# Scores, convolution and output weights of a fused attention and gated MLP kernel, rearranged

## Chip, core and metric

The kernel runs on one core of one Trainium2 chip. The metric is device time in microseconds; three runs of the kernel before gave 685.39, 685.6 and 686.19 us, median 685.6.

## The reference, cut to what matters

Eight batches, each of 576 positions. Local attention over 8 heads of 64, then a gate made by a causal convolution of 5 taps, then a spatial MLP:

```python
scores = (q @ k.T) / sqrt(64)          # heads 0-3: keys 0..31 back; heads 4-7: every 4th key, 0..127 back
attn = softmax(where(mask, scores, -1e9))
x = attn @ v                            # [8, 576, 512], heads side by side
gate_pre = sum(conv_w[k] * x shifted by 4 - k positions for k in range(5))
x = (sigmoid(gate_pre) * (x @ moe_w_val)) @ moe_w_out
h = relu(x @ moe2_w_in); u, v = halves of h
v = layernorm(v over channels)
y = (u * (w_spatial @ v + b_spatial)) @ moe2_w_out
```

## The kernel before

**Layout.** The features lie on partitions, 128 at a time, the 576 positions in the free dimension. Heads go in pairs: pair p (0 to 3) holds two heads, one in partitions 0 to 63, one in 64 to 127. The positions of heads 4 to 7 are permuted on the host so that their dilated window is a plain one of 32. A pair has 18 query blocks of 32, and each needs 64 keys only.

**Scores** (`a_scores`, L278): for each of the 18 blocks and each head one matmul with 64 rows of contraction, 32 query columns and 64 keys, float32. Block `BLOCK[e][x]` goes to block column x (0 to 8) and partition half e of one PSUM tile `s_ps` with one buffer; head h goes to partitions 64 e + 32 h. So four positions of the array are used: rows 0 to 63 with column strips 0 and 64, rows 64 to 127 with strips 32 and 96. `a_max` (L295) adds the mask on VectorE, out of PSUM, and takes the maxima; `a_exp`, `a_sum` and `a_trans` finish the softmax. Behind the first batch `a_trans` (L341) transposes 32x32 blocks on VectorE and moves them into the tile `pt` with 16 transfers on SP's queue, by the four runs of block columns in `RUNS` (L38).

**PV and convolution.** `a_pv` (L380) multiplies `pt` with the values into the PSUM tile `o_ps` (one buffer, two banks), and ScalarE copies it to `xt`, which has four zero columns in front. `a_split` makes two float32r parts of `xt` for the products. `a_conv` (L413) makes the gate's input on VectorE, one `tensor_scalar` (L425) and four `scalar_tensor_tensor` (L427), each reading `xt` shifted by one more position. For pairs 2 and 3 the copy also undoes the permutation.

**MLP.** A batch has 37 steps on TensorE (`mlp_steps`, L461): 8 `val`, 5 `vstep`, 8 `ustep`, 8 `spstep` (spatial), 8 `outstep`. Each accumulates products of float32r parts into one of four PSUM buffers of the tag `m`, which VectorE or ScalarE must drain before it is used again. `spstep` is drained by VectorE (`ru`, L569). Each `vstep` puts its result in a buffer of the tag `v`, of which there are two; `vnorm` releases it, one step later. The last spatial matmuls of a step use the fifth v tile.

**Weights.** They come as float64. `load_w` brings them in, `from64` (L621) makes float32 of them with one ScalarE and four VectorE instructions, and a split makes two parts with one ScalarE cast and one GpSimd subtraction. The output weights `wo` come in four tiles through four buffers of the tag `raw`, which hold the spatial weights before; their float32 form uses the two buffers of tag `v`.

**Order.** `PRELUDE` lists what comes first. `FIRST` (L112) gives the weight work of the first batch a place among the 37 steps, and `attention_events` (L444) gives the attention of the next batch its places: PV of pair n stands at `pv_place(n)`, the scores two PVs ahead, the split 1 step behind PV (4.3 for pair 0), the convolution 0.2 behind that. All events are sorted by place and traced in that order. A scheduler then orders each engine's instructions by this order and by when it reckons operands and buffers to be ready; from the second batch on, matmuls stay in the order traced, and `in_order` pins an instruction behind the one traced before it on its engine. Queues of the engines and of SP are static: an instruction that waits holds up those behind it.

Of the kernel before, what the change touches and what calls it, by code (L numbers as in the profile page):

```python
# [8 lines left out]
F32 = mybir.dt.float32  # L9
# [23 lines left out]

BLOCK = [
    [3 * x if x < 6 else 3 * (x - 6) + 1 for x in range(NS)],
    [3 * (x + 3) + 1 if x < 3 else 3 * (x - 3) + 2 for x in range(NS)],
]
RUNS = [(0, 0, 6), (0, 6, 9), (1, 0, 3), (1, 3, 9)]  # L38

SCALE = 1.0 / float(D) ** 0.5  # L40

# [89 lines left out]
    (11.6, ("split_sp", 3)),  # L131
    (11.61, ("split_sp", 1)),
    (11.7, ("split_sp", 4)),
    (12.6, ("load_w", "wo", 0)),
    (14.2, ("w_f32", "wo", 0)),
    (14.21, ("split_out", "wo", 0)),
    (15.2, ("w_f32", "wo", 1)),
    (15.21, ("split_out", "wo", 1)),
    (15.3, ("load_w", "wo", 1)),
    (17.2, ("w_f32", "wo", 2)),  # L140
    (17.21, ("split_out", "wo", 2)),
    (18.2, ("w_f32", "wo", 3)),
    (18.21, ("split_out", "wo", 3)),
]


# [5 lines left out]
def attention_gated_mlp_kernel(  # L152
# [71 lines left out]
    def chunk(c):  # L224
        return slice(c * 128, c * 128 + 128)

    def by_slot(ap):
        return ap.rearrange("p (j k) -> p j k", k=SW)

    qk_t, vv_t, early = {}, {}, {}
    s_t, e_t, mx_t, sm_t, x_t, tt = {}, {}, {}, {}, {}, {}
    xh, xl = {}, {}

    def early_tile(p):
# [41 lines left out]
    def a_scores(b, p):  # L278
        t = qk_t.pop((b, p))
        s = ps_s.tile([128, 1024], F32, tag="s", name="s_ps")  # L280
        for i in range(2 * NS):
            x, e = divmod(i, 2)
            n = BLOCK[e][x]
            cols = slice(SW * x, SW * x + SW)
            keys = slice(QB * n, QB * n + SW)
            for h in range(2):
                r = slice(64 * h, 64 * h + 64)
                q = t[r, KEYS + QB * n:KEYS + QB * n + QB]
                o = 64 * e + QB * h
                matmul(s[o:o + QB, cols], q, t[r, keys], True, True)  # L290
        if b or p >= 2:
            load_qk(b, p + 2)
        s_t[b, p] = s

    def a_max(b, p):  # L295
        s = s_t.pop((b, p))
        if b == 0 and p == 1:
            e = by_slot(boot[:, 0:S])
        elif b == 0 and p == 2:
            e = by_slot(act.tile([128, S + 64], F32, tag="gh0", name="e_t")[:, 0:S])  # L300
        else:
            e = act.tile([128, NS, SW], F32, tag="e", name="e_t")
        in_order(b == 1 and p < 2, nc.vector.tensor_tensor(
            out=e, in0=by_slot(s[:, 0:S]), in1=mask_sb[:, p // 2], op=ALU.add
        ))
        mx = rot.tile([128, NS, 1], F32, tag="mx", name="mx")
        nc.vector.tensor_reduce(out=mx[:, :, 0], in_=e, axis=AX.X, op=ALU.max)
        if b < 2:
            nc.vector.tensor_scalar(out=mx, in0=mx, scalar1=-SCALE, scalar2=None, op0=ALU.mult)
            mx_t[b, p] = mx  # L310
        else:
            nc.vector.tensor_tensor(out=e, in0=e, in1=mx.to_broadcast([128, NS, SW]), op=ALU.subtract)
        e_t[b, p] = e
# [27 lines left out]
    def a_trans(b, p):  # L341
# [30 lines left out]
        for q, lo, hi in RUNS:  # L372
            j, i = divmod(BLOCK[q][lo], 3)
            for c in range(2):
                k = 32 * (i + c)
                for h in range(2):
                    r = 64 * q + 32 * h
                    nc.sync.dma_start(out=pt[k:k + 32, i, h, j:j + hi - lo], in_=t[r:r + 32, c, lo:hi])  # L378

    def a_pv(b, p):  # L380
# [8 lines left out]
        for j in range(NJ):  # L389
            c = 512 * (j // 3) + 96 * (j % 3)  # L390
            for h in range(2):
                r = slice(64 * h, 64 * h + 64)
                matmul(o[r, c:c + 96], u[:, j, r], pt[:, :, h, j], True, True)
        o = o.rearrange("p (a c) -> p a c", a=2)[:, :, 0:HS]
        if b or p >= 2:
            load_vv(b, p + 2)
        if p < 2:
# [14 lines left out]

    def a_conv(b, p):  # L413
        xt = x_t.pop((b, p))
        t = act.tile([128, S], F32, tag=f"tt{p}", name="tt")
        tt[b, p] = t
        if b == 0 and p == 0:

            nc.scalar.activation(out=t, in_=xt[:, 0:S], func=ACTF.Copy, scale=cw[:, p, 0:1])
# [196 lines left out]
    def in_order(late, ins):  # L616

        if late:
            tc.keep_in_program_order(ins)

    def from64(dst, src, late=False):  # L621


        hi, lo = src[..., 1], src[..., 0]
        di = dst.bitcast(I32)
        nc.scalar.activation(out=dst, in_=_f(hi), func=ACTF.Abs)
        in_order(late, nc.vector.tensor_scalar(
            out=dst, in0=dst, scalar1=LEAST, scalar2=MOST, op0=ALU.max, op1=ALU.min
        ))
        nc.vector.tensor_scalar(  # L630
            out=di, in0=di, scalar1=3, scalar2=0x3FFFFFF8, op0=ALU.logical_shift_left, op1=ALU.bitwise_and
        )
        nc.vector.scalar_tensor_tensor(
            out=di, in0=hi, scalar=-0x40000000, in1=di, op0=ALU.bitwise_and, op1=ALU.bitwise_or
        )
        nc.vector.scalar_tensor_tensor(
            out=di, in0=lo, scalar=29, in1=di, op0=ALU.logical_shift_right, op1=ALU.bitwise_or
        )

    def conv_w_f32():  # L640
        from64(cw.rearrange("p c k -> p (c k)"), cw_raw)
# [1 line left out]
    def w_f32(key, u):  # L643
        if key == "wo":
            wide[key, u] = rot.tile([128, DM], F32, tag="v", name="wo_f32")
            from64(wide[key, u], raw.pop((key, u)))
            return
        if key not in wide:
            if key == "wv":
# [182 lines left out]
```

## Time and profile before

| | |
|---|---|
| median of three runs | 685.6 us (685.39 to 686.19) |
| the profiled execution, span from first to last instruction | 682.8 us |
| TensorE busy | 655.3 us (96%) |
| VectorE busy | 433.5 us (63%) |
| ScalarE busy | 301.1 us (44%) |
| GpSimd busy | 329.7 us (48%) |
| mean granted TensorE clock | 0.995 |

The profiled execution's own time is its span; the runs' times take in what lies around it. In the rows below PE is TensorE's matmul, PEld its weight load, DVE is VectorE, ACT ScalarE, POOL GpSimd, SPq SP's queue. `out<-in` are tiles by the program's names, `x72` a count of instructions; L210 is the line of the helper that issues every product, so its rows are told apart by their tiles. A matmul's duration holds its passage through the array; matmuls overlap, and their spacing is read from their starts. [...]

### The profile page before, as it was taken

To read this page: it belongs to the slowest core of one execution; us is meant where nothing else is said; L and a number is where in the kernel's file an instruction comes from. 1 tells how busy PE (TensorE), PEld (TensorE's weight loads), DVE (VectorE), ACT (ScalarE), POOL (GpSimd) and SP (SyncE) were. 2 spreads that over 40 slices of the span, in tenths; PEclk is the share of its full clock that TensorE was granted. 3 is DMA by queue.
4 is the path that set the end of the run, shared out by engine and by line. 5 is a ranking of instruction groups with operands and counts; after the bars stand their busy time and mean duration, and the time that the engine had idled before them with its cause. 6 is when DMAs were issued, how large, how long until landed. Compare 5 with 4: busy or idle time off the path is not lost.

```text
span 682.8 us, 16818 instructions
## 1 busy us (share of the span) xinstructions
PE 655.3 (96%) x6804; PEld 600.1 (88%) x6804; DVE 433.5 (63%) x740; ACT 301.1 (44%) x687; POOL 329.7 (48%) x370
## 2 busy tenths in 40 slices
PE   3699999989999999999999999999999999999998
PEld 3356678879899998999899999999899989999998
DVE  5998868884776466655686466656676577632510
ACT  4865666643353334443344334342444334442422
POOL 2675788562544355433645255343735355424420
PEclk9899999999999999999999999999999999999999
DMA  8961125313222421233122422233022411010002
GB/s 338 399 198 40 49 78 180 113 40 118 75 76 75 147 79 36 77 106 112 54 77 78 143 82 65 70 107 114 23 78 85 139 42 35 20 64 14 1 1 70
DMA packets 43553, 63.13 MB, mean 92 GB/s; under 512 B 16850, under 2 KB 32594, under 8 KB 42964
## 3 DMA queue, kind: packets, MB, share of 16 engines
q1 hardware_dynamic: 34260, 52.62, 24.5%
q10 hardware_dynamic: 9216, 9.44, 4.0%
q8 instruction: 54, 0.88, 0.5%
q14 instruction: 23, 0.19, 0.1%
HBM read 44.33 MB, written 9.44 MB: 79 GB/s over the span
## 4 chain that ended last, share of the span: by engine, by line
PE 82%; DVE 8%; DMA 3%; ACT 3%; POOL 2%; issue 1%; SPq 1%; ACTq 0%; POOLq 0%
PE sp_ps L210 15%; PE val_ps L210 14%; PE v_ps L210 14%; PE out_ps L210 13%; PE u_ps L210 13%; PE o_ps L210 5%; PE s_ps L210 4%; PE w_ps L210 3%; DVE tt L427 3%; DMA out<-ob 2%; SPq L378 1%; DMA raw<-in_w_mid_t 1%; ACT e_t L324 1%; POOL boot L351 1%; PE t_ps L360 1%
## 5 line engine op out<-in xcount | busy, mean ns | idle before, releaser
L427 DVE SCALAR_TENSOR_TENSOR tt<-xt,cw,tt 128x576 f32<-128x576 f32 x124 | 125.6, 1013 | 1.3
L210 PE MATMUL sp_ps<-wsp_h,vh 128*128 128x288 f32 x320 | 93.9, 298 | 2.6 <-DVE ru L569 1.8
L204 POOL TENSOR_TENSOR gl<-tt,gh 128x288 fp32r<-128x288 f32 x64 | 56.1, 884 | 70.7 <-ACT gh L203 70.6
L204 POOL TENSOR_TENSOR g2l<-ru,g2h 128x288 fp32r<-128x288 f32 x64 | 54.2, 857 | 63.1 <-ACT g2h L203 62.9
L210 PE MATMUL out_ps<-g2h,wout_h 128*128 128x288 f32 x256 | 76.5, 299 | 1.0 <-DVE ru L569 1.0
L210 PE MATMUL u_ps<-gh,w_h 128*128 128x288 f32 x256 | 76.6, 299 | 0.6 <-ACT ru L550 0.6
L210 PE MATMUL out_ps<-g2l,wout_h 128*128 128x288 f32 x256 | 75.8, 296 | 0.0
L210 PE MATMUL u_ps<-gl,w_h 128*128 128x288 f32 x256 | 75.5, 295 | 0.0
L210 PE MATMUL u_ps<-gh,w_l 128*128 128x288 f32 x256 | 75.4, 295 | 0.0
L210 PE MATMUL sp_ps<-wsp_l,vh 128*128 128x288 f32 x256 | 75.4, 294 | 0.0
L210 PE MATMUL sp_ps<-wsp_h,vl 128*128 128x288 f32 x256 | 75.4, 294 | 0.0
L210 PE MATMUL out_ps<-g2h,wout_l 128*128 128x288 f32 x256 | 75.3, 295 | 0.0
L204 POOL TENSOR_TENSOR xl<-xt,xh 128x576 fp32r<-128x576 f32 x28 | 49.5, 1769 | 49.6 <-ACT xh L203 49.6
L210 PE MATMUL val_ps<-xh,wval_h 128*128 128x288 f32 x224 | 66.7, 298 | 0.2 <-ACT ob L581 0.2
L210 PE MATMUL val_ps<-xh,wval_l 128*128 128x288 f32 x224 | 66.1, 295 | 0.0
L210 PE MATMUL val_ps<-xl,wval_h 128*128 128x288 f32 x224 | 65.9, 294 | 0.0
L538 POOL TENSOR_TENSOR vl<-v_t,vh 128x512 fp32r<-128x512 f32 x32 | 41.5, 1298 | 49.4 <-ACT vh L529 49.3
L210 PEld LDWEIGHTS sp_ps<-wsp_h,vh 128*128 128x128 f32 x320 | 60.0, 188 | 3.7 <-DVE ru L569 2.0
L210 PE MATMUL v_ps<-w_h,gh 128*128 128x512 f32 x160 | 59.6, 397 | 0.0
L210 PE MATMUL v_ps<-w_l,gh 128*128 128x512 f32 x160 | 59.2, 394 | 0.0
L203 ACT CAST g2h<-ru 128x288 fp32r<-128x288 f32 x64 | 27.4, 431 | 72.0 <-DVE ru L569 71.9
L425 DVE TENSOR_SCALAR tt<-xt,cw 128x576 f32<-128x576 f32 x31 | 18.2, 587 | 64.6 <-ACT xt L400 50.7
(137 smaller groups left out, 1681.1 us busy)
## 6 DMA issues: line engine op xcount, KB each, us to landing
qk_t<-in_qk SPq DMA_DIRECT2D x30, 592.0 KB, 5.3
vv_t<-in_vv SPq DMA_DIRECT2D x30, 384.0 KB, 3.9
out<-ob ACTq DMA_DIRECT2D x64, 144.0 KB, 1.8
pt<-et SPq DMA_DIRECT2D x224, 24.0 KB, 1.8
raw<-in_w_in SPq DMA_DIRECT2D x4, 1024.0 KB, 8.5
pt<-et SPq DMA_DIRECT2D x224, 12.0 KB, 2.0
raw<-in_w_mid_t SPq DMA_DIRECT2D x2, 1024.0 KB, 6.0
raw<-in_w_val SPq DMA_DIRECT2D x2, 1024.0 KB, 13.7
```

Of the source, the lines that this page charges most:

```text
L203: nc.scalar.copy(out=hi, in_=raw)
L204: nc.gpsimd.tensor_tensor(out=lo, in0=raw, in1=_f(hi), op=ALU.subtract)
L210: m = nc.tensor.matmul(o, a, r, start=start, stop=stop)
L324: nc.scalar.activation(out=e[:, x, :], in_=e[:, x, :], func=ACTF.Exp, scale=SCALE, bias=mx[:, x, :], accum_out=sm[:, x, :])
L351: nc.gpsimd.tensor_tensor(out=padded[r, lo:hi, k:k + SW], in0=e[r, lo:hi], in1=sm[r, lo:hi].to_broadcast([64, hi - lo, SW]), op=ALU.mult,)
L360: nc.tensor.transpose(ps[:, chunk(i)], padded[:, 3 * g + i, :], ident_sb)
L378: nc.sync.dma_start(out=pt[k:k + 32, i, h, j:j + hi - lo], in_=t[r:r + 32, c, lo:hi])
L425: nc.vector.tensor_scalar(out=t, in0=xt[:, 0:S], scalar1=cw[:, p, 0:1], scalar2=None, op0=ALU.mult)
L427: nc.vector.scalar_tensor_tensor(out=t, in0=xt[:, k:k + S], scalar=cw[:, p, k:k + 1], in1=t, op0=ALU.mult, op1=ALU.add)
L538: nc.gpsimd.tensor_tensor(out=low["v"][:, i], in0=v, in1=_f(h), op=ALU.subtract)
```

## The change

The block columns of the second partition half are renumbered, so that for block columns 6 to 8 both halves can swap the two heads' strips (`_swapped`); the score loop issues x and x + 6 side by side; three block columns lie in each 256 columns of PSUM, and block columns 6 to 8 in the second bank. The convolution of pairs 0 and 1, in all batches but the first, reads `o_ps`; instead of shifting its input it writes to the output tile shifted by j positions, and the tile has four columns more, set to zero by GpSimd. The ten entries for the output weights stand three steps earlier in `FIRST`, and all four VectorE instructions of their `from64` are pinned.

```diff
@@ -33,9 +33,15 @@
 
 BLOCK = [
     [3 * x if x < 6 else 3 * (x - 6) + 1 for x in range(NS)],
-    [3 * (x + 3) + 1 if x < 3 else 3 * (x - 3) + 2 for x in range(NS)],
+    [3 * x + 2 if x < 6 else 3 * (x - 3) + 1 for x in range(NS)],
 ]
-RUNS = [(0, 0, 6), (0, 6, 9), (1, 0, 3), (1, 3, 9)]
+RUNS = [(0, 0, 6), (0, 6, 9), (1, 0, 6), (1, 6, 9)]
+
+
+def _swapped(b, x):
+
+    return int(b > 0 and x >= 6)
+
 
 SCALE = 1.0 / float(D) ** 0.5
 
@@ -131,16 +137,16 @@
     (11.6, ("split_sp", 3)),
     (11.61, ("split_sp", 1)),
     (11.7, ("split_sp", 4)),
-    (12.6, ("load_w", "wo", 0)),
-    (14.2, ("w_f32", "wo", 0)),
-    (14.21, ("split_out", "wo", 0)),
-    (15.2, ("w_f32", "wo", 1)),
-    (15.21, ("split_out", "wo", 1)),
-    (15.3, ("load_w", "wo", 1)),
-    (17.2, ("w_f32", "wo", 2)),
-    (17.21, ("split_out", "wo", 2)),
-    (18.2, ("w_f32", "wo", 3)),
-    (18.21, ("split_out", "wo", 3)),
+    (9.60, ("load_w", "wo", 0)),
+    (11.20, ("w_f32", "wo", 0)),
+    (11.21, ("split_out", "wo", 0)),
+    (12.20, ("w_f32", "wo", 1)),
+    (12.21, ("split_out", "wo", 1)),
+    (12.30, ("load_w", "wo", 1)),
+    (14.20, ("w_f32", "wo", 2)),
+    (14.21, ("split_out", "wo", 2)),
+    (15.20, ("w_f32", "wo", 3)),
+    (15.21, ("split_out", "wo", 3)),
 ]
 
 
@@ -224,13 +230,16 @@
     def chunk(c):
         return slice(c * 128, c * 128 + 128)
 
+    def by_bank(ap):
+        return ap.rearrange("p (a x) k -> p a (x k)", a=3)
+
     def by_slot(ap):
         return ap.rearrange("p (j k) -> p j k", k=SW)
 
 
 
     qk_t, vv_t, early = {}, {}, {}
-    s_t, e_t, mx_t, sm_t, x_t, tt = {}, {}, {}, {}, {}, {}
+    s_t, e_t, mx_t, sm_t, o_t, x_t, tt = {}, {}, {}, {}, {}, {}, {}
     xh, xl = {}, {}
 
     def early_tile(p):
@@ -278,15 +287,15 @@
     def a_scores(b, p):
         t = qk_t.pop((b, p))
         s = ps_s.tile([128, 1024], F32, tag="s", name="s_ps")
-        for i in range(2 * NS):
-            x, e = divmod(i, 2)
+        for x, e in ((x, e) for i in range(6) for e in range(2) for x in (i, i + 6) if x < NS):
             n = BLOCK[e][x]
-            cols = slice(SW * x, SW * x + SW)
+            c = 256 * (x // 3) + SW * (x % 3)
+            cols = slice(c, c + SW)
             keys = slice(QB * n, QB * n + SW)
             for h in range(2):
                 r = slice(64 * h, 64 * h + 64)
                 q = t[r, KEYS + QB * n:KEYS + QB * n + QB]
-                o = 64 * e + QB * h
+                o = 64 * e + QB * (h ^ _swapped(b, x))
                 matmul(s[o:o + QB, cols], q, t[r, keys], True, True)
         if b or p >= 2:
             load_qk(b, p + 2)
@@ -301,7 +310,8 @@
         else:
             e = act.tile([128, NS, SW], F32, tag="e", name="e_t")
         in_order(b == 1 and p < 2, nc.vector.tensor_tensor(
-            out=e, in0=by_slot(s[:, 0:S]), in1=mask_sb[:, p // 2], op=ALU.add
+            out=by_bank(e), in0=s[:, 0:768].rearrange("p (a c) -> p a c", a=3)[:, :, 0:3 * SW],
+            in1=by_bank(mask_sb[:, p // 2]), op=ALU.add,
         ))
         mx = rot.tile([128, NS, 1], F32, tag="mx", name="mx")
         nc.vector.tensor_reduce(out=mx[:, :, 0], in_=e, axis=AX.X, op=ALU.max)
@@ -374,7 +384,7 @@
             for c in range(2):
                 k = 32 * (i + c)
                 for h in range(2):
-                    r = 64 * q + 32 * h
+                    r = 64 * q + 32 * (h ^ _swapped(b, lo))
                     nc.sync.dma_start(out=pt[k:k + 32, i, h, j:j + hi - lo], in_=t[r:r + 32, c, lo:hi])
 
     def a_pv(b, p):
@@ -392,6 +402,8 @@
                 r = slice(64 * h, 64 * h + 64)
                 matmul(o[r, c:c + 96], u[:, j, r], pt[:, :, h, j], True, True)
         o = o.rearrange("p (a c) -> p a c", a=2)[:, :, 0:HS]
+        if b and p < 2:
+            o_t[b, p] = o
         if b or p >= 2:
             load_vv(b, p + 2)
         if p < 2:
@@ -412,8 +424,22 @@
 
     def a_conv(b, p):
         xt = x_t.pop((b, p))
-        t = act.tile([128, S], F32, tag=f"tt{p}", name="tt")
-        tt[b, p] = t
+        t = act.tile([128, S + 4], F32, tag=f"tt{p}", name="tt")
+        tt[b, p] = t[:, 0:S]
+        if b and p < 2:
+            o = o_t.pop((b, p))
+            nc.gpsimd.memset(t[:, S:], 0.0)
+            for k in range(TAPS - 1, -1, -1):
+                j = TAPS - 1 - k
+                to = t[:, j:j + S].rearrange("p (a c) -> p a c", a=2)
+                if j == 0:
+                    nc.vector.tensor_scalar(out=to, in0=o, scalar1=cw[:, p, k:k + 1], scalar2=None, op0=ALU.mult)
+                else:
+                    nc.vector.scalar_tensor_tensor(
+                        out=to, in0=o, scalar=cw[:, p, k:k + 1], in1=to, op0=ALU.mult, op1=ALU.add
+                    )
+            return
+        t = t[:, 0:S]
         if b == 0 and p == 0:
 
             nc.scalar.activation(out=t, in_=xt[:, 0:S], func=ACTF.Copy, scale=cw[:, p, 0:1])
@@ -618,7 +644,7 @@
         if late:
             tc.keep_in_program_order(ins)
 
-    def from64(dst, src, late=False):
+    def from64(dst, src, late=False, last=False):
 
 
         hi, lo = src[..., 1], src[..., 0]
@@ -627,15 +653,15 @@
         in_order(late, nc.vector.tensor_scalar(
             out=dst, in0=dst, scalar1=LEAST, scalar2=MOST, op0=ALU.max, op1=ALU.min
         ))
-        nc.vector.tensor_scalar(
+        in_order(last, nc.vector.tensor_scalar(
             out=di, in0=di, scalar1=3, scalar2=0x3FFFFFF8, op0=ALU.logical_shift_left, op1=ALU.bitwise_and
-        )
-        nc.vector.scalar_tensor_tensor(
+        ))
+        in_order(last, nc.vector.scalar_tensor_tensor(
             out=di, in0=hi, scalar=-0x40000000, in1=di, op0=ALU.bitwise_and, op1=ALU.bitwise_or
-        )
-        nc.vector.scalar_tensor_tensor(
+        ))
+        in_order(last, nc.vector.scalar_tensor_tensor(
             out=di, in0=lo, scalar=29, in1=di, op0=ALU.logical_shift_right, op1=ALU.bitwise_or
-        )
+        ))
 
     def conv_w_f32():
         from64(cw.rearrange("p c k -> p (c k)"), cw_raw)
@@ -643,7 +669,7 @@
     def w_f32(key, u):
         if key == "wo":
             wide[key, u] = rot.tile([128, DM], F32, tag="v", name="wo_f32")
-            from64(wide[key, u], raw.pop((key, u)))
+            from64(wide[key, u], raw.pop((key, u)), True, True)
             return
         if key not in wide:
             if key == "wv":
```

## Rows read from the trace of the kernel before

**Rows 1.** The page's first line.
```profile
span 682.8 us, 16818 instructions
```

**Rows 2.** Busy time by stretches; columns: stretch, its length, each engine's busy us (instructions), PEclk, DMA share, GB/s.
```profile
311.93:387.87 75.94, 75.94 (x843) 71.97 (x842) 48.44 (x88) 30.40 (x60) 35.21 (x41) 1.00 0.28 86
53.68:159.45 105.77, 98.67 (x953) 83.64 (x951) 86.02 (x133) 60.82 (x164) 72.15 (x67) 1.00 0.28 86
```

**Rows 3.** TensorE in order of time, from 343.2; columns: start us, us.
```profile
343.38 1.21 PE L210 MATMUL o_ps<-pt,vv_t 128*64 128x96 f32 x24
344.52 1.21 PE L210 MATMUL s_ps<-qk_t 64*32 64x64 f32 x72
345.66 0.40 PE L210 MATMUL u_ps<-gh,w_h 128*128 128x288 f32 x1
```

**Rows 4.** The same from 344.53, ended at 344.60, 344.65, 344.71; durations min/median/max (ns).
```profile
344.52 0.26 PE L210 MATMUL s_ps<-qk_t 64*32 64x64 f32 x4
...
344.52 0.32 PE L210 MATMUL s_ps<-qk_t 64*32 64x64 f32 x8
...
344.52 0.37 PE L210 MATMUL s_ps<-qk_t 64*32 64x64 f32 x12
...
L210 PE MATMUL s_ps<-qk_t x72: 216/216/240, 344.5 to 345.5; 64*32 64x64 f32 x72
```

**Rows 5.** Busy time by stretches of s_ps alone; columns: PE, PEld, DVE, PEclk, DMA.
```profile
53.68:159.45 105.77, 8.39 (x360) 6.13 (x360) 4.50 (x6) 1.00 0.28 86
0.00:53.68 53.68, 9.35 (x360) 8.01 (x360) 2.95 (x4) 0.94 0.82 309
```

**Rows 6.** Waits of TensorE, 53.68 to 159.45; columns: us in total, times, longest.
```profile
PE sp_ps L210 <- DVE ru L569: 1.8, 1, 1.8
PE w_ps L210 <- POOL wiu_l L204: 1.2, 1, 1.2
PE out_ps L210 <- DVE ru L569: 1.0, 1, 1.0
```

**Rows 7.** Groups of VectorE; columns: busy us, mean ns of one | idle before, releaser.
```profile
L427 DVE SCALAR_TENSOR_TENSOR tt<-xt,cw,tt 128x576 f32<-128x576 f32 x124 | 125.6, 1013 | 1.3
...
L303 DVE TENSOR_TENSOR e_t<-s_ps,mask_sb 128x576 f32<-128x576 f32 x31 | 23.2, 748 | 4.3 <-PE s_ps L210 4.2
...
L425 DVE TENSOR_SCALAR tt<-xt,cw 128x576 f32<-128x576 f32 x31 | 18.2, 587 | 64.6 <-ACT xt L400 50.7 <-POOL gh L487 12.0 <-ACT xt L398 1.8
```

**Rows 8.** VectorE from 353.5 and TensorE from 361, in order of time.
```profile
353.54 0.81 DVE L427 SCALAR_TENSOR_TENSOR tt<-xt,cw,tt 128x576 f32<-128x576 f32 x1
...
361.01 0.30 PE L210 MATMUL o_ps<-pt,vv_t 128*64 128x96 f32 x2
```

**Rows 9.** Busy time of wo_f's instructions alone; columns: DVE, ACT, POOL, PEclk, DMA.
```profile
119.00:146.50 27.50, 10.10 (x16) 5.10 (x8) 5.21 (x4) 1.00 0.26 81
```

**Rows 10.** VectorE in order of time, the drains at 128.96 and 139.65.
```profile
128.96 0.42 DVE L569 TENSOR_TENSOR ru<-sp_ps,ru 128x288 f32<-128x288 f32 x1
...
139.65 0.44 DVE L569 TENSOR_TENSOR ru<-sp_ps,ru 128x288 f32<-128x288 f32 x1
```

**Rows 11.** Busy time of all engines, 95.95 to 122.41; columns as in rows 2.
```profile
95.95:122.41 26.46, 25.82 (x229) 23.13 (x228) 23.94 (x36) 16.44 (x32) 21.21 (x18) 1.00 0.49 153
```

**Rows 12.** VectorE at 110.2 and 121, TensorE at 122.4, in order of time.
```profile
110.25 0.68 DVE L509 TENSOR_TENSOR v_t<-v_ps,v_lo 64x512 f32<-64x512 f32 x1 [1.73 <-POOL vl L538]
...
120.87 0.69 DVE L534 TENSOR_TENSOR vh<-v_t,vh 64x512 fp32r<-64x512 f32 x1
...
122.45 0.30 PE L210 MATMUL sp_ps<-wsp_h,vh 128*128 128x288 f32 x1
```

**Rows 13.** SP's queue in order of time, from 107.5.
```profile
107.58 0.36 SPq L601 DMA_DIRECT2D raw<-in_w_out  x1
...
111.62 0.36 SPq L601 DMA_DIRECT2D raw<-in_w_out  x1
```

**Rows 14.** Busy time of all engines, 30.5 to 37.4; columns as in rows 2.
```profile
30.50:37.40 6.90, 5.20 (x6) 2.18 (x7) 6.76 (x11) 4.16 (x14) 4.83 (x5) 0.51 0.50 194
```

## The prediction

> **What bounds the kernel now.** I began with the span, 682.8 us [rows 1], and cut it into stretches. In a whole batch of the steady part TensorE is busy for 75.94 of 75.94 us [rows 2]; VectorE, ScalarE and GpSimd are busy for 48, 30 and 35 us of it. So there a microsecond off TensorE's own work is a microsecond off the end, and one off another engine is nothing. The stretch that holds the first batch is different: TensorE is busy for 98.67 of 105.77 us [rows 2], and that is where other engines can be felt.
>
> The second look was at the scores inside a steady batch. TensorE goes from the last PV matmul of a pair to the scores at 344.52 and on to the next product at 345.66 [rows 3], so one execution of the scores costs 1.14 us. It has 72 matmuls (36 calls, each in two passes). How they start shows what limits them [rows 4]: 4 have begun by 344.60, 8 by 344.65, 12 by 344.71, and the stretch they cover grows from 0.26 to 0.32 to 0.37 us. So they go in rounds of four, one on each tile in use, one round every 0.055 us, 18 rounds an execution; the longest single matmul takes 0.24 us, so starts inside a round lie (0.26 - 0.24) / 3, some 7 ns apart. Nor does a column get dearer with more tiles in flight: PV, on two tiles, takes 1.14 us for 12 rounds of 96 columns, 0.99 ns a column; the scores, on four, 1.14 us for 18 rounds of 64, again 0.99 ns [rows 3].
>
> **Part 1, scores on eight tiles.** The head in rows 0 to 63 and the one in rows 64 to 127 swap their column strips for block columns 6 to 8, and the loop issues x and x + 6 side by side. For i = 0 to 2 eight tiles are in turn: 8 calls, 2 passes, 2 rounds instead of 4. For i = 3 to 5 there is no x + 6, and it stays at four tiles. So 6 + 6 = 12 rounds instead of 18: 6 x 0.055 = 0.33 us less for each execution, provided a round of eight lasts as long as one of four; eight starts 7 ns apart need 0.056 us, which just fits.
>
> There are 32 executions, 360 / 72 = 5 of them before 53.68 and 5 in the first batch's stretch [rows 5], so 22 in the steady part: 22 x 0.33 = 7.3 us, all on the path. In the first batch one of the five lies among waits of w_ps for wiu_l, 1.2 us [rows 6], and I count 4 x 0.33 = 1.3 us. Before 53.68 other engines set the pace, and I count one execution, 0.3 us. Sum 8.9 us. Bounds: nothing, if the pairs of tiles block each other; 32 x 0.33 = 10.6 us, if all lie on the path.
>
> [...]
>
> The scores now lie in three pieces of 192 columns; the mask addition reads the same 576 elements in one instruction as before. The transposed copies keep their 16 transfers a pair, in runs of 6, 3, 6, 3 for 6, 3, 3, 6. Nothing for both.
>
> **Part 2, convolution out of PSUM.** Fourteen convolutions (seven batches, pairs 0 and 1) read o_ps instead of xt. Now one costs 587 + 4 x 1013 = 4.64 us of VectorE; the nearest row with a PSUM operand of the same size is the mask addition, 748 ns, so 5 x 0.75 = 3.74 us [rows 7]. I take that: 0.9 us of VectorE less each. Bounds for one instruction are the means of the two SBUF forms, 587 and 1013 ns. On the path in the steady part: 0, under TensorE's 75.94 us; were that cover gone, the 0.9 us would count. GpSimd gets one small memset more each, also covered. The new wait: o_ps has one buffer, and its next PV must now wait for the last convolution step as well as ScalarE's copy. Pair 1 has the shortest distance: its last step starts at 353.54 and takes 0.81 us, the next PV starts at 361.01 [rows 8], a margin of 6.7 us. Even five steps at 1013 ns are only 0.4 us more than now. Were it late, the products behind PV on TensorE would wait.
>
> **Part 3, output weights three steps ahead.** Each of four tiles moves with everything it issues: one load on SP's queue, an absolute value and a cast on ScalarE, four VectorE steps, one GpSimd subtraction. Together 10.1 us of VectorE, 5.1 of ScalarE, 5.2 of GpSimd [rows 9], 5.1 us a tile one after another. What goes: the third spatial product is drained at 128.96 and the fourth only at 139.65 [rows 10], with steps for two of these tiles between. TensorE waits for these drains, 1.8 and 1.0 us [rows 6]. Without output weights there, both go: -2.8 us.
>
> What comes: the target, 95.95 to 122.41, has VectorE busy 23.94 of 26.46 us and GpSimd 21.21 [rows 11]. Two convolutions there give back 1.8 us, so VectorE has about 4.3 us for 10.1; the rest slips behind 122.4, where two of the four tiles are worked on now, but should be clear of 130. More delicate are the two buffers of tag v, which the tiles now share with the v tiles. The fifth v tile already waits for one (VectorE idle 1.73 us until GpSimd's vl) and its last step ends at 121.56; TensorE wants it at 122.45 [rows 12], a margin of 0.9 us. An output-weight tile ahead of it in program order (11.20 against 12) may take that buffer for 5.1 us. So a new wait of TensorE before the 13th spatial matmul of between 0 and 4.2 us; neither end is nearer, and I take the middle, 2.1. The held VectorE steps stand behind the v steps traced before them, and behind them can queue the fifth v tile's steps, for which the spatial product waits. On SP's queue pt transfers are behind these loads: today 4.0 us pass between two loads, 107.58 to 111.62, with pt transfers between [rows 13], and the same slots must be waited for; I count nothing more, 0 to 4.0 us at worst, inside the same wait.
>
> **Sum.** 682.8 - 8.9 - 2.8 + 2.1 = 673.2 us of span. The median of the three runs, 685.6, stands 2.8 us above this execution's span, so 676.0 us.
>
> **Rivals.** *Half the gain (0.12).* The rows fit two orders: passes alternating over all tiles, or first passes of four calls and then their second passes. In the second, starting in order, the next four overlap only with the second passes: 3 rounds for eight calls in place of 2, half the saving lost, 27 x 0.165 = 4.5 us: 680.5. For it: rounds of four would look the same. Against: PV's rounds hold two. [...]
>
> *No gain from the scores (0.12).* Each column strip is now used by both row halves, which no row of before shows; if they take turns, the round of eight lasts two rounds: 676.0 + 8.9 = 684.9. Against: columns cost the same on two and four tiles. [...]
>
> *Slower (0.08).* The fifth v tile waits for two output tiles in turn and for the second one's load: 2 x 5.1 + 4.0 - 0.9 = 13.3 us, in place of 2.1. [...] For it: two buffers, static queues. Against: program order puts only one output tile ahead. It decides once the new wait exceeds about 8.9 + 2.8 + 1.4 = 13.1 us.
>
> **Numbers.** The forecast, eight tiles in full, has 0.68, its own range 673.9 to 678.1 by the wait of 0 to 4.2 us. The range of 8 in 10 takes in the first rival, and below it other waits of the first batch that may shrink too: 671.5 to 682.0. A measurement here tells 0.2% (1.4 us) from no change. Faster: 0.68 + 0.12 and a quarter of the second rival, 0.83. Within 0.2%: the middle of the second, 0.08. Slower: its rest and the third, 0.09.
>
> **What would show it.** Scores from PV's end to the next product in 0.81 us, eight starts to a round; steady batches of 74.6 us; no wait of sp_ps and out_ps for ru of 1 us or more; convolution steps on o_ps near 750 ns. Wrong would be: scores still at 1.14 us (second rival), 0.97 (first), or a wait of sp_ps beyond 13 us at the first spatial tile (third).

## The result, and the profile after

Four runs of the changed kernel have a median of 676.75 us (675.97 to 677.35), four of the kernel before 685.88 (685.39 to 686.19): ratio 0.987, 95% interval 0.986 to 0.9885. The forecast was 676.0. In a second set of runs the ratio was 0.987 (0.9855 to 0.9885). The time came out as forecast, but the terms behind it did not: the scores brought about half of theirs, the convolution, put at nothing, brought microseconds in the first batch, and the output weights gained only together with the others. Where kernels are compared below, the ratios leave out two slow executions, one of the scores alone (905 us) and one of the output weights alone (2227 us).

First the page's first line, then busy time by stretches as in [rows 2], PEclk the granted share of TensorE's full clock: a whole batch of the steady part, and the stretch of the first batch (first `val` to the next batch's first `val`).

```profile
span 675.4 us, 16859 instructions
```
```profile
307.49:382.64 75.15, 75.15 (x843) 71.26 (x841) 47.41 (x87) 30.94 (x61) 33.76 (x43) 1.00 0.29 86
54.40:157.20 102.80, 98.31 (x954) 82.69 (x952) 81.62 (x132) 60.87 (x165) 68.96 (x69) 1.00 0.29 90
```

Against [rows 1, 2] the span is 7.4 us shorter: +0.7 before the first `val` (54.40 for 53.68), -3.0 in the first batch, -1.4 in the batch behind it (76.54 to 75.15), -0.8 in each of the next four and -0.4 in the seventh. TensorE still fills the steady batch; all of its gain is TensorE's own work. In the first batch 2.6 us of the 3.0 are less idle time of TensorE (7.1 to 4.5).

TensorE in order of time (columns as in [rows 3]): the scores now take 340.79 - 339.84 = 0.95 us to the next product (0.96 in most executions), for 1.14 before and 0.81 forecast.

```profile
338.70 1.21 PE L216 MATMUL o_ps<-pt,vv_t 128*64 128x96 f32 x24
339.84 1.03 PE L216 MATMUL s_ps<-qk_t 64*32 64x64 f32 x72
340.79 0.40 PE L216 MATMUL u_ps<-gh,w_h 128*128 128x288 f32 x1
```

And how they start, the same view ended at 339.89, 339.97, 340.08 and 340.16, to be set beside [rows 4]:

```profile
339.84 0.29 PE L216 MATMUL s_ps<-qk_t 64*32 64x64 f32 x8
...
339.84 0.34 PE L216 MATMUL s_ps<-qk_t 64*32 64x64 f32 x16
...
339.84 0.45 PE L216 MATMUL s_ps<-qk_t 64*32 64x64 f32 x32
...
339.84 0.54 PE L216 MATMUL s_ps<-qk_t 64*32 64x64 f32 x34
```

Eight matmuls go where four went, 32 have begun within 0.24 us, in four rounds of eight; the step from 16 to 32 lengthens the stretch by 0.11 us, two rounds of 0.055. Then comes the surprise: in the next 0.08 us only two more begin. In the starts themselves the 17th call still begins at 0.266 us behind the first (its turn was at 0.247, one round of 0.056 behind the last start on its tile) and its second pass at 0.322; the 18th begins only at 0.330, where its turn was at 0.253, and the following ones about 17 ns apart, where rounds of eight use a call every 14.

TensorE's waits in the first batch, for [rows 6]:

```profile
PE w_ps L216 <- ACT wiu_h L209: 1.1, 1, 1.1
PE sp_ps L216 <- DVE ru L595: 0.8, 1, 0.8
PE out_ps L216 <- DVE ru L595: 0.6, 1, 0.6
...
PE sp_ps L216 <- DVE vh L560: 0.3, 1, 0.3
```

The two waits for `ru` are half of what they were (2.8 to 1.4 us). The new wait for the fifth v tile is there, but small. The tile did come late: its first VectorE step at 117.93 (110.25 in [rows 12]), its last at 127.12, and output-weight steps run up to 143.27:

```profile
117.93 0.67 DVE L535 TENSOR_TENSOR v_t<-v_ps,v_lo 64x512 f32<-64x512 f32 x1
...
127.12 0.87 DVE L560 TENSOR_TENSOR vh<-v_t,vh 64x512 fp32r<-64x512 f32 x1 [0.69 <-ACT vh L555]
...
143.27 0.68 DVE L662 SCALAR_TENSOR_TENSOR wo_f<-raw,wo_f 128x512 int32<-128x512 int32 x1
```

TensorE waits only 0.3 us for it because the scheduler put PV and scores in front of those spatial matmuls, between 125.14 and 128.05:

```profile
127.39 0.33 PE L216 MATMUL s_ps<-qk_t 64*32 64x64 f32 x12
128.05 0.40 PE L216 MATMUL sp_ps<-wsp_h,vh 128*128 128x288 f32 x1 [0.33 <-DVE vh L560]
```

VectorE's groups for [rows 7]: the convolution from `o_ps` costs 811 + 4 x 805 ns = 4.03 us, for 4.64 before and 3.74 forecast. The mask addition stayed at 744 ns.

```profile
L438 DVE SCALAR_TENSOR_TENSOR tt<-o_ps,cw,tt 128x576 f32<-128x576 f32 x56 | 45.1, 805 | 0.0
...
L312 DVE TENSOR_TENSOR e_t<-s_ps,mask_sb 128x576 f32<-128x576 f32 x31 | 23.1, 744 | 4.8 <-PE s_ps L216 4.7
...
L436 DVE TENSOR_SCALAR tt<-o_ps,cw 128x576 f32<-128x576 f32 x14 | 11.4, 811 | 11.3 <-POOL gh L513 10.5 <-ACT xt L410 0.7
```

### The profile page after: what moved, and what is told of

It reads as the page before. It is cut to its first block, busy times and chain, and to the rows that moved or that the text cites. A ratio compares the mean times of both kernels' runs of the same rounds, so it can differ in the third digit from the quotient of the medians.

```text
span 675.4 us, 16859 instructions
## 1 busy us (share of the span) xinstructions
PE 649.4 (96%) x6804; PEld 594.6 (88%) x6804; DVE 423.5 (63%) x740; ACT 302.7 (45%) x687; POOL 319.0 (47%) x384
## 4 chain that ended last, share of the span: by engine, by line
PE 86%; DVE 5%; POOL 3%; DMA 2%; SPq 2%; ACT 1%; issue 1%; DVEq 0%; POOLq 0%
PE sp_ps L216 16%; PE v_ps L216 15%; PE out_ps L216 15%; PE val_ps L216 15%; PE u_ps L216 15%; PE o_ps L216 5%; PE s_ps L216 4%; POOL boot L361 2%; SPq L388 1%; PE w_ps L216 1%; POOL tt L449 1%; DMA raw<-in_w_mid_t 1%; DVE tt L453 1%; DMA pt<-et 1%; ACT e_t L334 0%
## 5 line engine op out<-in xcount | busy, mean ns | idle before, releaser
L210 POOL TENSOR_TENSOR gl<-tt,gh 128x288 fp32r<-128x288 f32 x64 | 52.3, 821 | 61.8 <-ACT gh L209 61.8
L210 POOL TENSOR_TENSOR xl<-xt,xh 128x576 fp32r<-128x576 f32 x28 | 46.2, 1650 | 50.3 <-ACT xh L209 50.3
L453 DVE SCALAR_TENSOR_TENSOR tt<-xt,cw,tt 128x576 f32<-128x576 f32 x68 | 64.9, 954 | 1.0
L209 ACT CAST gh<-tt 128x288 fp32r<-128x288 f32 x64 | 27.4, 431 | 70.5 <-DVE tt L508 69.4
```

Source lines behind the costliest of these rows:

```text
L209: nc.scalar.copy(out=hi, in_=raw)
L210: nc.gpsimd.tensor_tensor(out=lo, in0=raw, in1=_f(hi), op=ALU.subtract)
L453: nc.vector.scalar_tensor_tensor(out=t, in0=xt[:, k:k + S], scalar=cw[:, p, k:k + 1], in1=t, op0=ALU.mult, op1=ALU.add)
```

## The experiments

Two questions: which part brings what, and why an execution of the scores takes 0.96 us.

### The parts, alone and in pairs

The scores alone (block numbering, `_swapped`, loop order and their readers):

```diff
...
+        for x, e in ((x, e) for i in range(6) for e in range(2) for x in (i, i + 6) if x < NS):
...
+                o = 64 * e + QB * (h ^ _swapped(b, x))
...
```

> The kernel before with the scores on eight tiles alone. Theory: the saving is in TensorE's own work in every batch, 1.14 to 0.96 us an execution as in the changed kernel, so 22 x 0.18 = 4.0 us in the steady batches and about 1 us in the first: 680.9 us, and both waits of sp_ps and out_ps for ru (2.8 us) stay. Rival: the waits of the first batch shrink through the scores too, because the matmuls are ordered anew: 678 us or less, and the other two parts bring nothing.

The convolution alone:

```diff
...
+                        out=to, in0=o, scalar=cw[:, p, k:k + 1], in1=to, op0=ALU.mult, op1=ALU.add
...
```

> The kernel before with the convolution of pairs 0 and 1 out of PSUM alone. Theory: VectorE gets 0.6 us shorter for each convolution but TensorE has no gap in a steady batch, so the time moves by 0.5 us at most in the first two batches: 685.2 to 686.0 us. Rival: the shorter convolutions in the first batch take away the waits for ru as well (2.8 us): 683 us.

The output weights alone, earlier and pinned:

```diff
-    (12.6, ("load_w", "wo", 0)),
...
+    (9.60, ("load_w", "wo", 0)),
...
+            from64(wide[key, u], raw.pop((key, u)), True, True)
...
```

> The kernel before with the output weights three steps ahead and held in order alone. Theory: the waits for ru shrink from 2.8 to about 1.4 us as in the changed kernel: 684.4 us. Rival: the fifth v tile's wait for its buffer costs as much or more, as the convolutions still take their full time on VectorE: 686 to 688 us.

Then the three pairs, each the changed kernel with one part put back (in `sw` the convolution, in `sc` the output weights, in `cw` the scores), and the changed kernel once more beside them:

```diff
sw
-                        out=to, in0=o, scalar=cw[:, p, k:k + 1], in1=to, op0=ALU.mult, op1=ALU.add
...
sc
-    (9.60, ("load_w", "wo", 0)),
...
+    (12.6, ("load_w", "wo", 0)),
...
cw
-        for x, e in ((x, e) for i in range(6) for e in range(2) for x in (i, i + 6) if x < NS):
+        for i in range(2 * NS):
...
```

> Scores on eight tiles plus the earlier, held output weights; the convolution as before. If the parts simply add, the medians of the first runs give 688.2 + 686.5 - 684.8 = 689.9 us. Theory: the eight-tile scores alone lost their gain because TensorE then waited for the output weights (wout, 2.8 + 1.1 us) and fell to half its clock behind that wait; the earlier output weights take that wait away, so no out_ps wait for wout over 0.5 us, a first batch of 102 to 105 us in place of 112.4, and 678 to 681 us. A wait for wout that stays, with 685 us or more, would refute it.

> Scores on eight tiles plus the convolution out of PSUM; output weights at their old places. If the parts add: 688.2 + 683.4 - 684.8 = 686.8 us. Theory: the output weights stay where they were, so a wait of out_ps for wout of 1 us or more and a stretch at half clock are still in the first batch, and it takes 684 to 687 us; steady batches of 75.15 us as in the changed kernel. Rival: the 1.8 us that the convolutions leave VectorE are enough to have the output weights in time, no such wait, 677 to 680 us.

> Convolution out of PSUM plus earlier, held output weights; scores as before on four tiles. If the parts add: 683.4 + 686.5 - 684.8 = 685.1 us. Theory: steady batches of 75.93 us, nothing gained there; the wait for pt (1.9 us) and the half clock behind it that the output weights alone brought come from where the scheduler put PV, and I expect them to be gone where the convolutions free VectorE: first batch of 103.5 to 105.5 us, 682 to 684.5 us. Rival: the wait for pt stays, 685 us or more.

> The changed kernel itself, beside the others on one chip: 675.5 to 677.5 us, a ratio to the kernel before of 0.986 to 0.990. Anything outside would mean that the ratios of this chip and of the first measurement cannot be set side by side.

What was measured (the first three and the last four in one set of runs each, with the kernel before in both); "first batch" and "steady batch" are read from each profile as above. A profile is of one execution. That of the output weights alone is the slowest of its kind (688.12 us, the others 684.33 to 687.79), so its first batch says too much.

| parts | median us | ratio (95%) | first batch us | steady batch us | last step of wo_f starts |
|---|---|---|---|---|---|
| none | 684.83, 684.72 | 1 | 105.77 | 75.94 | 142.99 |
| convolution | 683.4 | 0.9975 (0.9965 to 0.9985) | 105.12 | 75.93 | 144.71 |
| output weights | 686.52 | 1.001 (0.9992 to 1.0027) | 108.94 | 75.94 | 147.02 |
| scores | 688.23 | 1.0041 (1.0028 to 1.0054) | 112.36 | 75.27 | 152.55 |
| convolution, weights | 682.21 | 0.9961 (0.9947 to 0.9975) | 102.76 | 75.93 | 141.41 |
| scores, weights | 681.34 | 0.9948 (0.9936 to 0.996) | 105.68 | 75.27 (one of 75.60) | 146.24 |
| scores, convolution | 685.13 | 0.9999 (0.9989 to 1.0009) | 110.06 | 75.18 | 147.69 |
| all | 676.15 | 0.987 (0.9855 to 0.9885) | 101.99 | 75.18 | 142.97 |

The steady batch depends on the scores (75.2 to 75.3 us with them, 75.9 without); the convolution moves it by 0.1 us at most. The first batch depends on all three, and the parts don't add there: the sum of the three single differences would be 0.26% slower, and all together are 1.3% faster. By the medians the output weights alone cost 1.7 us, by the ratio 0.7, neither clear of zero (in the profiled execution 3.2 of first batch); with the convolution they bring 1.2, with the scores 6.9, and with both other parts 9.0. The convolution brings 1.4 alone, and 5.2 where scores and weights are there already.

The waits of TensorE in the first batch with the scores alone show why that kernel is slower:

```profile
PE out_ps L216 <- POOL wout_l L210: 2.8, 1, 2.8
PE sp_ps L216 <- DVE ru L579: 2.0, 1, 2.0
PE u_ps L216 <- ACT ru L560: 1.4, 1, 1.4
PE out_ps L216 <- ACT wout_h L209: 1.1, 1, 1.1
```

The static order now had the output weights late (first VectorE step 127.70, last 152.55), and TensorE waited for them. Busy time by stretches of that kernel (columns as in [rows 2]) shows the second price:

```profile
134.00:136.00 2.00, 2.00 (x18) 2.00 (x17) 2.00 (x3) 0.62 (x1) 1.94 (x3) 1.00 0.52 191
136.00:138.00 2.00, 0.56 (x5) 0.32 (x3) 2.00 (x2) 0.00 (x0) 1.55 (x1) 1.00 0.09 20
140.00:142.00 2.00, 2.00 (x11) 2.00 (x10) 2.00 (x4) 0.95 (x2) 0.84 (x1) 0.50 0.10 25
139.68:143.09 3.41, 3.41 (x16) 2.96 (x16) 3.41 (x4) 0.95 (x2) 2.13 (x3) 0.50 0.10 23
154.00:156.00 2.00, 0.39 (x1) 0.39 (x2) 2.00 (x2) 0.62 (x1) 2.00 (x2) 0.50 0.00 0
156.00:158.00 2.00, 2.00 (x10) 2.00 (x10) 2.00 (x4) 0.00 (x0) 1.32 (x1) 0.50 0.00 0
153.33:160.16 6.83, 4.55 (x18) 4.43 (x19) 6.83 (x8) 1.32 (x3) 3.99 (x3) 0.50 0.06 15
```

VectorE is busy without a break. TensorE is busy for only 0.56 and 0.39 of 2 us, then works at a granted clock of 0.50: 10 or 11 matmuls in 2 us for 18 at 1.00. The two stretches at 0.50 are 139.68 to 143.09 and 153.33 to 160.16. In them TensorE is busy for 3.41 + 4.55 = 8.0 us, and its products of 288 columns start 0.24 us apart for 0.13 before, so an estimated 3.6 us are lost. All waits of that first batch sum to 9.8 us against 7.0 before, 2.8 more. Both together, 6.4 us, are about the 6.6 that it is longer; that the scores themselves got shorter, by 5 x 0.18 = 0.9 us, leaves some 1 us without an account. With the output weights alone there was a wait of another kind,

```profile
PE o_ps L210 <- DMA pt<-et: 1.9, 1, 1.9
```

and the granted clock fell to 0.50 behind it (131.62 to 138.44) and behind an earlier wait of 1.2 us (87.24 to 90.66):

```profile
128.00:130.00 2.00, 0.11 (x6) 0.02 (x1) 1.55 (x4) 2.00 (x11) 1.47 (x2) 1.00 0.07 17
...
134.00:136.00 2.00, 2.00 (x29) 1.55 (x27) 1.97 (x6) 1.97 (x4) 0.00 (x0) 0.50 0.53 117
```

Scores with weights and scores with convolution have such a stretch too (0.50 in 132 to 134; in 148 to 150 and from 160.5); the kernel before, the changed one, the convolution alone and convolution with weights have none in the first batch. The length of a single wait does not decide it: behind one of 1.1 us the clock fell to 0.50 (scores with weights), behind one of 1.8 it stayed at 1.00 (the kernel before). Of the expectations, `sw` held in its mechanism (no wait for wout) and narrowly missed its numbers (681.34 us for 678 to 681, a first batch of 105.68 for 102 to 105), `sc` held (a wait of out_ps for wout_h of 1.8 us stayed), and `cw` held in its time, with a first batch 0.7 us better than expected. For `s_only` both times fell, as the first batch lost more than the steady batches gained (75.27 for 75.94 us). For `w_only` the time was the rival's, 686 to 688, but its mechanism was the smaller part: the v tile's wait is 0.9 us, that for pt 1.9, and the waits for `ru` on VectorE went completely. For `c_only` the rival's time of 683 was right, and its mechanism in half: of the waits for `ru` 1.3 of 2.8 us stay, and others, of val_ps for tt (1.3) and for the output weights (1.2), are in their place. The convolution alone brings 0.65 us in the first batch and 0.6 in the one behind it.

### The hold

```diff
-            from64(wide[key, u], raw.pop((key, u)), True, True)
+            from64(wide[key, u], raw.pop((key, u)))
```

> The changed kernel without the four pins on the output weights' VectorE steps (one of them was pinned before already); their places stay three steps ahead. Theory: the places do the work and the pins decide only how the VectorE steps fall between ru and the v steps; first batch of 102.5 to 106 us, 676 to 680 us. Rival (without the pins the scheduler puts the steps late again and TensorE waits for wout): a wait for wout of 1 us or more, over 681 us.

677.87 us, ratio 0.9888 (0.9863 to 0.9912), first batch 102.85 us (102.80 and 101.99 with the pins), no wait for wout; the intervals overlap. The earlier places do the work; a worth of the pins was not seen. (In the kernel before none of the four was pinned for the output weights.)

### Why 0.96 us

The author's conjecture is that the calls don't reach TensorE fast enough once the ones at hand are used up. If so, the order in which eight-tile and four-tile calls come must matter. First the four-tile calls in front:

```diff
-        for x, e in ((x, e) for i in range(6) for e in range(2) for x in (i, i + 6) if x < NS):
+        for x, e in ((x, e) for i in (3, 4, 5, 0, 1, 2) for e in range(2) for x in (i, i + 6) if x < NS):
```

> The changed kernel with the order of the score blocks turned: i = 3, 4, 5 (four tiles) ahead of 0, 1, 2 (eight tiles). Same matmuls, same tiles. Theory, supply of instructions: in the changed kernel the first 32 matmuls start in four full rounds of eight, then a gap of 84 ns follows with one start in it and calls come only one every 17 ns; if that is because the instructions that had gathered are used up, a slow start on four tiles (28 ns a call) lets the supply catch up, and the scores take 0.84 us or less instead of 0.96: 676.8 - 27 x 0.12 = 673.5 us. Rival, the tiles: eight tiles at once slow one another; the order does not matter: 0.96 us, 676.8 us.

678.4 us, ratio 0.9907 (0.9889 to 0.9924): 340.93 - 339.94 = 0.99 us an execution, longer and not shorter.

```profile
339.94 1.06 PE L216 MATMUL s_ps<-qk_t 64*32 64x64 f32 x72
340.93 0.40 PE L216 MATMUL u_ps<-gh,w_h 128*128 128x288 f32 x1
```

So slow calls in front give no head start, and both expectations fell. The starts tell more. In this order the 19th and the 20th call are the first behind the 16th whose tiles are idle; they begin 0.349 and 0.365 us behind the first start. In the changed kernel the same two, on busy tiles, begin at 0.347 and 0.364, behind the 18th at 0.330. In the kernel before rounds of four need even the 17th only at 0.47, and no pause shows. By these starts, as an estimate, the calls behind the 17th are to be had from about 0.33 us on, one every 17 ns, in either order, and the eight-tile calls should be spread:

```diff
+        for x, e in ((x, e) for i in (0, 3, 1, 4, 2, 5) for e in range(2) for x in (i, i + 6) if x < NS):
```

> The changed kernel with the score loop in the order i = 0, 3, 1, 4, 2, 5, so that calls on eight tiles and calls on four alternate; the same calls, tiles and addresses. Theory (calls reach TensorE at about 17 ns each once the first 16 are used up, with 82 to 84 ns lost at that point): the first 16 calls now last 0.28 us, the 17th starts at about 0.35, 20 calls at 17 ns bring the last to 0.68 and its second pass to 0.75; with the 0.15 us to the next product 0.88 to 0.92 us an execution, 674.3 to 676 us in all. Rival (the eight-tile calls themselves are slower than thought, or passes run in two halves): the order changes nothing, 0.96 us or more, 676 us or more.

The execution is as expected, 341.97 - 341.07 = 0.90 us, the 19th and 20th call again begin at 0.348 and 0.365, and steady batches are 74.90 us:

```profile
341.07 0.97 PE L216 MATMUL s_ps<-qk_t 64*32 64x64 f32 x72
341.97 0.40 PE L216 MATMUL u_ps<-gh,w_h 128*128 128x288 f32 x1
```

Yet the whole takes 677.14 us, ratio 0.9883 (0.986 to 0.9905): the scheduler placed other work differently in the first batch, 104.74 us in place of 101.99 and 102.80, with a wait of sp_ps for ru of 1.8 us and a granted clock of 0.50 in 140 to 142. The last kernel keeps the old order up to pair 1 of the third batch, and with it all of the first batch's order:

```diff
+        for x, e in ((x, e) for i in ((0, 3, 1, 4, 2, 5) if (b, p) >= (2, 2) else range(6)) for e in range(2) for x in (i, i + 6) if x < NS):
```

> The changed kernel with the alternating score order only from pair 2 of the third batch of attention on, so that all that is issued in the first batch stands in the changed kernel's order. Theory: the alternating order is worth 0.055 us in each of 22 steady executions, 1.2 us, and it lost that in the first batch only because the scheduler placed the other work differently there (104.7 against 102.8 us): with the first batch as it was, 102 to 103 us for it, steady batches of 74.9 us, 674.3 to 675.6 us, ratio 0.985. Rival: what the steady executions gain is given back by a wait elsewhere or the first batch differs from run to run: 676 us or more.

675.56 us, ratio 0.9866 (0.985 to 0.9883). First batch and steady batch in its profile:

```profile
54.35:156.31 101.96, 97.66 (x954) 82.50 (x953) 82.08 (x132) 60.64 (x165) 68.99 (x69) 1.00 0.30 91
231.20:306.14 74.94, 74.94 (x843) 71.02 (x842) 47.31 (x88) 31.00 (x61) 33.65 (x43) 1.00 0.30 86
```

Both parts of the expectation held (the first batch by 0.04 us better), and it is the fastest kernel of the study; 0.6 us below the changed kernel is less than their intervals can tell apart, so the gain is shown by the stretches, not by the medians.

To measure the spacing of the calls by itself, the eight-tile calls were issued four times over:

```diff
+        for x, e in ((x, e) for i in (0, 1, 2) * 4 + (3, 4, 5) for e in range(2) for x in (i, i + 6) if x < NS):
```

> The changed kernel with the calls of i = 0, 1, 2, those on eight tiles, issued four times over (the same results written again), 72 calls more an execution. Theory (supply of 17 ns a call): 72 x 16.7 to 17 ns = 1.2 us more, 2.16 to 2.18 us an execution. Rival one (rounds of eight at 0.056 us, 14 ns a call, limit it): 1.01 us more, 1.97 us. Rival two (the 82 ns are lost again at every 16 calls): 2.4 to 2.55 us.

The kernel takes 800.8 us in its one run. Behind 190 us two executions have no stop; they take 2.44 us (479.69 - 477.25), 1.48 more for 72 calls: 20.5 ns a call. That is in the range of rival two, and its mechanism holds in kind. In both, calls begin 16.7 ns apart in runs of 17, from 0.331 to 0.598 and from 0.659 to 0.926 us behind the first, with 61 ns between two runs, so the pause returns, though it costs 44 ns and not 82 (second passes run meanwhile, so no gap between any two starts shows it). A run and its pause make 328 ns for 17 calls, 19.3 ns a call; what makes 20.5 of it was not followed up. But most executions stop altogether; one that does, and one that does not:

```profile
337.98 2.17 PE L216 MATMUL s_ps<-qk_t 64*32 64x64 f32 x188
342.47 0.56 PE L216 MATMUL s_ps<-qk_t 64*32 64x64 f32 x28 [2.33 <-issue]
...
477.25 2.51 PE L216 MATMUL s_ps<-qk_t 64*32 64x64 f32 x216
479.69 0.40 PE L216 MATMUL val_ps<-xh,wval_h 128*128 128x288 f32 x1
```

After 188 matmuls TensorE sits for 2.3 us and waits for nothing that the profile shows. Behind 190 us, 17 of 22 executions have such a stop, of 0.7 to 3.3 us from start to start, behind 106 to 212 matmuls, and three more a shorter one; in the whole span the group of s_ps has 40.4 us of it. The page lists a queue q8 of the kind instruction, with its packets, MB and share; the first line is the changed kernel's, the second this one's:

```profile
q8 instruction: 54, 0.88, 0.6%
```
```profile
q8 instruction: 90, 1.47, 0.8%
```

0.59 MB more for 32 x 72 = 2304 calls is 256 bytes a call, or, as an estimate, 64 for each of the 26100 - 16859 = 9241 instructions more (four a call: two passes of a load and a matmul). So a call of the scores has four instructions for the 14 ns that it takes in rounds of eight. That the stops are a lack of instructions is the author's estimate from this trace; no view names it. All 20 of them behind 190 us end 1.2 to 1.6 us after a packet of this queue has ended, and from one to the next TensorE has executed a multiple of 256 instructions (512, 768 or 1280, within 2), which at the estimated 64 bytes each is a whole number of the queue's packets (16384 bytes, all 54 of the changed kernel's).

The short pause of the changed kernel is another matter. That the calls set it and not the tiles is shown by the starts: in three orders, on idle tiles or busy ones, the 19th and 20th call begin at the same times, 0.347 to 0.349 and 0.364 to 0.365 us behind the first. What holds the calls back there no row tells.

## Why the prediction was right, and where it was not

**Scores, -8.9 us.** The mechanism held: eight tiles run side by side, a round of eight lasts as long as one of four, 0.055 us. The step that failed is "12 rounds instead of 18: 6 x 0.055 = 0.33 us less": it took for granted that a call starts as soon as its turn comes, and the 18th started at 0.330 us in place of 0.253. 0.18 to 0.19 us was measured, 22 x 0.18 = 4.0 us in the steady part for 7.3. The rows of before could not show it, since rounds of four use a call every 28 ns and the 17 ns measured behind the pause lie between 14 and 28; the text bounded the round from the array's side alone. The first rival's time for an execution, 0.97 us, came true for a reason that it did not name: first passes of eight are followed at once by their second passes, so its order is refuted. The second rival, two row halves taking turns in a strip, is refuted by the rounds of eight. Whether these need the second PSUM bank, into which the change moved block columns 6 to 8, no run shows.

In the first batch the 1.3 us are not found as such: set on convolution and weights, the scores change that stretch from 102.76 to 102.80 or 101.99 us. Over the whole kernel they then bring 682.21 - 676.15 = 6.1 us.

**Convolution, 0 on the path.** Right in the steady part (75.93 for 75.94 us). The term was mis-sized: 4.03 us, not 3.74, for 805 ns a step and not 748. The step that failed is the 0 for the first batch, where the prediction gave it only room on VectorE: there it is worth 0.65 us alone, and the medians go down by 4.3 us where it joins the weights (686.52 to 682.21) and by 5.2 where it joins scores and weights (681.34 to 676.15). Its wait for `o_ps` did not show: no wait of PV for a convolution step is in the profile, pair 1 ends at 349.5 in the profile after, and the next PV starts at 356.09.

**Output weights, -2.8 + 2.1 us.** The stretch became 3.0 us shorter, the prediction's net for it was -2.0 (0.7 here, 1.3 by the scores). The waits for `ru` on VectorE went by half, and completely with the weights alone and with convolution and weights. The new wait for the v tile was 0.3 us of an estimated 0 to 4.2, for a reason that the step did not see: the order of TensorE's work moved too. That the steps would be "clear of 130" was wrong, and with it "Without output weights there, both go": only the first two tiles moved (VectorE steps from 111.83 to 124.18), while the eight steps of the other two still run from 128.79 to 143.27, as they did before from 130.20 to 142.99. So the weights did not leave the stretch in which TensorE waits for `ru`, and what halved these waits no run isolates. The forecast took each part's worth as its own; the pairs show that the same weights part brings nothing or 9 us, as the other parts stand.

**Sum.** Of the forecast 9.6 us of span, 7.3 were to come in the steady part, 2.0 in the first batch, 0.3 before it. What came is 5.1 (4.0 of it scores), 3.0 and -0.7, so 675.4 us and not 673.2. The 2.8 us from span to median were 1.4 here (676.75 - 675.4), which made up for most of it. The steady part missed by 2.2 us, the start lost 1.0, and the first batch gave 1.0 more than forecast: that 676.0 came so close to 676.75 is in good part luck.

**Slower, the third rival.** Its mechanism did not occur: TensorE's wait for the fifth v tile was 0.3 us, not 13.3. A low clock did come, in other kernels: in the scores alone and the weights alone the granted clock was 0.50 in or behind TensorE's waits of 1.2 to 2.8 us (0.51 in [rows 14]), and neither is faster than before (688.23 and 686.52 us for 684.83).

## What to carry to other kernels

When small matmuls are spread over more tiles, look at how far apart the calls start and not only at their columns: the 14 ns a call of rounds of eight were out of reach here behind the 17th call, where 17 ns were measured, and spreading the fast calls among slower ones gave back a third of the loss (0.96 to 0.90 us, with 0.81 forecast). Where order comes from a scheduler, a part measured alone in the crowded stretch says little about it in company; measure the parts in pairs, and read the steady part and the crowded stretch apart. A wait of one to three microseconds on TensorE may have to be priced with the clock that it comes back at: here the granted clock fell to 0.50 in or behind waits of 1.1 to 2.8 us in five kernels, and not behind waits of 1.8 and 1.9 us in two others.

## What the runs showed of the hardware

- In the changed kernel matmuls on eight tiles started 6 to 7 ns apart, in rounds of 0.055 us behind a first one of 0.080, 32 starts in 0.24 us. On four tiles, in the kernel before, the spacing and the rounds were the same.
- In the changed kernel the float32 calls (two passes each) behind the 17th began about 17 ns apart, the first of them at 0.330 us behind the first call; the 19th and 20th began at 0.347 to 0.349 and 0.364 to 0.365 us in three orders. With 72 calls more they began 16.7 ns apart in runs of 17, with 61 ns between runs.
- In the kernel with repeated calls TensorE stopped within the scores for up to 3.3 us at a time. All 20 stops behind 190 us lay multiples of 256 TensorE instructions apart (512, 768 or 1280, within 2), and each ended 1.2 to 1.6 us after a packet of the instruction queue, whose packets have 1.47 MB / 90 = 16 KB. The profile names no wait for them.
- VectorE's steps on `o_ps` in PSUM took 776 to 817 ns, all 56; the same steps on `xt` in SBUF before took 801 to 2055. No run tells what stretches the latter.
- The granted clock fell to 0.50 in or behind waits of TensorE of 1.1 to 2.8 us in the first batch of five of the kernels built here (the scores and the weights alone, the scores with either other part, the alternating order), and from the first batch on in the one with repeated calls. It did not fall behind waits of 1.8 us in the kernel before and 1.9 us in the one without pins.
